# Earlier row copies, six products of zeros and an earlier request for small row transfers in a fused scan and two-layer network kernel

## The chip, the cores and the metric

The kernel runs on one core of a Trainium2 chip. The metric is device time in microseconds, from several executions, of which the median is given; the lower the better. A profiled execution records what each engine did and when: TensorE (PE, products, with its weight loads as PEld), VectorE (DVE), ScalarE (ACT), GpSimd (POOL) and SyncE (SP), which issues the DMA transfers.

## The reference

Three computations stand in a row: a gated linear recurrence over 768 tokens (4 batches, 8 heads, head dimension 32, state 16), a network with token mixing (1024 wide, squared ReLU, a sigmoid gate), and a second network (2048 wide, with h - tanh(h)).

```python
log_a = np.log(np.clip(a, 1e-06, 1.0))
cum = np.cumsum(la, axis=-1)                       # within a chunk
L = np.exp(cum[:, :, :, None] - cum[:, :, None, :]) * causal
M = np.einsum('bhin,bhjn->bhij', Cc, Bc) * L
y = M @ x + (C @ state) * exp(cum)                 # per chunk
state = decay_full * state + sum(B x decay_from_j)
...
xk = mu_k * x + (1.0 - mu_k) * x_prev;  xr = mu_r * x + (1.0 - mu_r) * x_prev
k = np.maximum(xk @ w_k, 0.0);  v = k * k @ w_v
r = 1.0 / (1.0 + np.exp(-(xr @ w_r)));  x = r * v
...
h = x @ w_in;  g = h - np.tanh(h);  out = g @ w_out
```

The third line and those with `y` and `state` are written short here.

## The kernel before

**Tiling.** The recurrence works in 12 groups of 256 tokens (4 chunks of 64 for all 8 heads). For a group k TensorE makes the exponents of the decays (`decays`, tile pd, line 442, for groups 0 and 1 line 438), ScalarE their exp (`decays_exp`, tile L), TensorE the score products (`scores`, pcb, L484), VectorE their product with the decays (`mask`, L544), TensorE the part that comes from the carried state (`inter`, L494), the state's additions (`terms`, L509) and the part within the chunk (`intra`, L516). VectorE carries the state on (`chain`, L558 and L561) and makes the scaled inputs bp (`weigh`, L457) and cp (`group_scale`, L428). ScalarE or VectorE copies the finished group from PSUM into xall (`group_out`). Both networks then work on 6 blocks of 512 tokens; each product is made as three products of high and low parts. The first network starts while the recurrence still runs.

**Weights.** The weights come as 64-bit numbers, 512 KB in one transfer (`fetch`, tile raw, L315), and are decoded into a high and a low part: one ScalarE square (keep, L322), four VectorE steps on raw and wd (L326, L329, L332, L335), a copy (wkh and the like, L364 or L366) and a subtraction (L341). There are two raw buffers; the first two fetches (W0 and W1 in the prediction, both from w_k) stand in the prologue.

**Decays of later groups.** The exponents of group k (from 2 on) are one product of `sr[:, k % 2]` with `rr[:, k % 2]`, 116 rows deep. Parts of both are fixed: sr is filled by GpSimd (`t_still`), and rows 0 to 111 of the two slots of rr by ScalarE (`causal`, then `spread`, one copy of 1024 columns each). The rest are rows of cumulated sums, which VectorE computes and SP writes out to `dcum`; `rows(k)` reads them back into sr and rr with two transfers (L399, L400). `prep_rows` reads such rows into kl (L404), from which TensorE (`scales_sum`, pc, L416) and an exp (er, L419) make the factors for cp and for the carried state (the carries).

**Order.** Each engine works its instructions off in the order in which they are written. The prologue's order is the list START, whose names stand for small functions: `W` is a weight fetch, `Db2` loads the third group's bct, `pr0` is `prep_rows` for the first batch's third group, `still` the fill of sr, `r0t` and `r0b` the copies into slot 0 of rr, `wa` 48 products of zeros on TensorE (`fill`, from the tile quiet), `d1` and `e1` the second group's decays and their exp, `sc1` its scores, `v0` the first group's visit (`inter`, `terms`, `intra`). All behind it is ordered by a greedy planner (`Plan.run`): each task has engines with modelled times, tasks that it follows, buffers (`Ring`) and a rank, and the planner always takes the task that can start first, among those ready the one of lowest rank. START_AT gives the time at which each engine is free in that model. The copies into slot 1 of rr are a planner task there, `filled` (2 ScalarE copies, rank of group 2), ahead of group 3's decays; `rows(2)` is one too. The first two blocks' decode is taken as ready from the model's start.

Of the kernel before, what the change touches and what calls it, by code (L numbers as in the profile page):

```python
# [16 lines left out]
P = 128  # L17
NB, NH, S, HD, NS = 4, 8, 768, 32, 16
NQ = NH // 2
L = 64  # L20
# [38 lines left out]

START = """  # L60
    qz tab Da Dla Dca Db0 Dx0 Db1 Dx1 Dnk Dnr seg mk wa c0t c1t c0b st mk2 tri
    cA lA cC lC sA ss h0s x0a cD lD x0b c1b ps pe d0 e0 dec dexp sD cum W Db2 W s0 x1a w0 x1b p0 m0 ob u0 h0 w1
    still heads r0t r0b spread sc1 d1 e1 v0 pr0 nu
""".split()

START_AT = dict(P=15.8, A=14.2, V=13.8, G=12.0, S=12.0, X=0.0, Y=0.0, Z=0.0)


def t_act(n, more=0.0):
    return 0.172 + n / 1200 + more
# [135 lines left out]
def chain_kernel(ctx, tc, xb, a, an, a0, bc, mu_k, mu_r, w_k, w_v, w_r, w_in, w_out, out):  # L208
# [14 lines left out]
    att = att_stack.enter_context(tc.tile_pool(name="att", bufs=1, side="right"))  # L223
    dram = ctx.enter_context(tc.tile_pool(name="dram", bufs=1, space=bass.MemoryType.DRAM))

    def fill(n):

        for _ in range(n):
            PE.matmul(acc[:, 0, 0:P], quiet, quiet, start=True, stop=True)  # L229

    def bank(name, shape=(2, BLK)):
        return pairs.tile([P, *shape], F32, tag="pair", name=name)
# [14 lines left out]
    dec = const.tile([P, NG, NQ, NC4], F32, name="dec")  # L247
    sums = const.tile([P, NU2 + 1], F32, name="sums")
    ones = const.tile([P, 1], F32, name="ones")
    quiet = const.tile([P, P], BF16, name="quiet")  # L250
    less = const.tile([P, NU2 + 1], F32, name="less")
    flag = const.tile([1, 1], I32, name="flag")

# [32 lines left out]
    for _ in range(NE):  # L286
# [2 lines left out]
    plan = Plan()  # L289
    add = plan.add  # L290
    R = dict(
        pair=Ring(3, ("pd", 1), ("pcb", 1), ("py", 0)), xb=Ring(3, 0, 1), bc=Ring(3, 0, 1, 2), rows=Ring(2, 0, 1), L=Ring(2, 0, 1), bp=Ring(2, 0, 1), cp=Ring(2, 0),
        er=Ring(2, 0), state=Ring(3, 0, 1), raw=Ring(2, *range(NW)), x=Ring(WORK["xh"]), l=Ring(WORK["l"], "p0"), h=Ring(WORK["h"], "p0", "p1"),
        s=Ring(WORK["s"], "p0"), acc=Ring(1), ob=Ring(3), raw2=Ring(2), f=Ring(WORK["f"], "p0", "p1"), wd=Ring(1), keep=Ring(2), wd2=Ring(1), keep2=Ring(2),
    )
# [102 lines left out]
    def rows(k):  # L398
        nc.sync.dma_start(out=f(sr[CUM:TOK, k % 2]), in_=dcum[k].rearrange("h x q c i -> (x q c) h i"))  # L399
        nc.sync.dma_start(out=f(rr[ROW:NR, k % 2]), in_=dcum[k].rearrange("h x q c i -> (h x) (q c) i"))  # L400

    def prep_rows(b, lo=0):
        d = dcum[NGB * b + lo // GT:NGB * (b + 1)].rearrange("k h x q c i -> (h x q) k (c i)")
        nc.sync.dma_start(out=f(kls[b % 2][TOK:ROW, lo:]), in_=d)  # L404
# [27 lines left out]
    def decays(k):  # L432
        pd = pds[k] = bank("pd")
        mt[k] = att.tile([P, 2, 2, NC4, L], F32, tag="L", bufs=2, name="L")
        if k < 2:
            for g in range(2):
                by = early["by", k][:, 2 * g:2 * g + 2].rearrange("p q c i -> p (q c i)")
                PE.matmul(pd[:, g], early["st"][:, k].rearrange("p h j -> p (h j)"), by, start=True, stop=True)
            return
        for g in range(2):  # L440
            by = rr[:, k % 2, 2 * g:2 * g + 2].rearrange("p q c i -> p (q c i)")
            PE.matmul(pd[:, g], sr[:, k % 2].rearrange("p h j -> p (h j)"), by, start=True, stop=True)
# [124 lines left out]
    def prologue(fetch1):  # L567
# [49 lines left out]
        def spread(out, lo, hi, cols, e):  # L617
            n = cols.stop - cols.start
            return lambda: copy(e, out[lo:hi], mk[lo:hi, cols].unsqueeze(2).to_broadcast([hi - lo, n, out.shape[-1]]))

        def causal(out, e):
            return lambda: copy(e, out[0:L], mk[0:L, 0:L].unsqueeze(1).to_broadcast([L, CQ, L]))

        def slot(k):
            return rr[:, k].rearrange("p q c i -> p (q c) i")
# [72 lines left out]
            V.memset(tbias, T2)  # L698
            G.memset(xall[:, :, 0:NB * (S + 1)].rearrange("p c (b s) -> p c b s", b=NB)[..., 0:1], 0.0)

        def rest():
            causal(slot(1), "A")()
            spread(slot(1), CUM, ROW, late, "A")()

        early["fill"] = rest
        fns = dict(
            qz=lambda: V.memset(quiet, 0.0), wa=warm(48), wc=warm(2), wd=warm(2), seg=t_seg,
            mk=t_mk, mk2=t_mk2, st=t_st, tri=t_tri, still=t_still, heads=t_heads, spread=t_spread,
# [1 line left out]
            c0t=causal(by[0], "V"), c1t=causal(by[1], "V"), c0b=spread(by[0], CUM, TOK, soon, "A"), c1b=spread(by[1], CUM, TOK, soon, "A"),  # L710
            h0s=spread(heads0.rearrange("p k (m n) -> p (k m) n", n=NS), CUM, TOK, pick, "A"),
            r0t=causal(slot(0), "A"), r0b=spread(slot(0), CUM, ROW, late, "A"),
            nu=t_nu,
            Da=load(ad, a0), Dla=load(la, a), Dca=load(ca, an), Dnk=load(mus["k"], mu_k), Dnr=load(mus["r"], mu_r), W=fetch1,
            Db0=lambda: bc_load(0), Db1=lambda: bc_load(1), Db2=lambda: bc_load(2), Dx0=lambda: xb_load(0), Dx1=lambda: xb_load(1),
# [3 lines left out]
            p0=lambda: scores(0), d0=lambda: decays(0), e0=lambda: decays_exp(0, True), d1=lambda: decays(1), e1=lambda: decays_exp(1, True),  # L719
            ps=scales0, pe=scales1, w0=lambda: weigh(0), w1=lambda: weigh(1), ob=lambda: out_bank(-1),  # L720
            u0=lambda: terms(0), m0=lambda: mask(0, True), h0=lambda: chain(0), s0=lambda: group_scale(0), sc1=lambda: scores(1), v0=lambda: visit(0),
            pr0=lambda: prep_rows(0, 2 * GT),
        )
        for o in START:
            fns[o]()
# [2 lines left out]
    def attention():  # L728

        D, E, MK, CH, GS, BPt, X, XL, BL, PSX, PS = ({} for _ in range(11))  # L730
        users = []

        def put(*args, **kw):
            t = add(*args, **kw)
            users.append(t)
            return t

        def at(k):
            return RANK_T * k

        def scales(b, lo, rank, after):
            take = [(R["pair"], ("pc", b))] + ([(R["er"], b)] if b else [])
            p = put(dict(P=0.62), lambda e: scales_sum(b, lo), after, rank, take, ins=4)
            PSX[b] = put(dict(A=t_act(S - lo)), lambda e: scales_exp(b, lo), [p], rank, uses=[take[0], (R["er"], b)], func="exp")
            return p

        PS[0] = scales(0, 2 * GT, at(2) - 2, [])
        E[1] = put(dict(Y=14.1), lambda e: None)
        filled = put(dict(A=2 * t_act(1024)), lambda e: early["fill"](), [], at(2))
        first_half, visited = None, put(dict(Z=14.8), lambda e: None)  # L750
        for k in range(1, NG + 1):
            if 2 <= k < NG:
                XL[k] = put(dict(S=0.47), lambda e, k=k: xb_load(k), [], at(k - 1.5), [(R["xb"], k)], dma=1.7)
                if k >= 3:
                    BL[k] = put(dict(S=0.47), lambda e, k=k: bc_load(k), [], at(k - 1.8), [(R["bc"], k)], dma=1.7)
                rw = put(dict(S=0.9), lambda e, k=k: rows(k), [], at(k - 1.2), [(R["rows"], k)], dma=0.2)
                D[k] = put(dict(P=0.7), lambda e, k=k: decays(k), [rw, filled if k == 3 else None], at(k) - 1.5, [(R["pair"], ("pd", k)), (R["L"], k)], [(R["rows"], k)], ins=4)
                E[k] = put(dict(A=t_act(1024)), lambda e, k=k: decays_exp(k), [D[k]], at(k) - 1.5, (), [(R["pair"], ("pd", k)), (R["L"], k)], func="exp")
                BPt[k] = put(dict(V=t_dve(GT)), lambda e, k=k: weigh(k), [XL[k]], at(k) - 1.5, [(R["bp"], k)], [(R["xb"], k)], port=True)
            b, g = divmod(k, NGB)  # L760
            if g == 0 and k < NG:
                pr = put(dict(S=0.45), lambda e, b=b: prep_rows(b), [PS.get(b - 2)], at(k - 1.2), (), dma=0.2)
                PS[b] = scales(b, 0, at(k) - 1.7, [pr])
            if k >= 2:
                j = k - 1
                take = ([(R["pair"], ("pcb", k))] if k < NG else []) + [(R["pair"], ("py", j))]
                use_a = [(R["cp"], j), (R["state"], j), (R["bc"], k)]
                use_b = [(R["pair"], ("py", j)), (R["L"], j), (R["xb"], j), (R["bp"], k), (R["xb"], k)]
                first_half = put(dict(P=(1.7 if j % NGB else 1.6) if k < NG else 0.65), lambda e, j=j: visit_a(j), [CH[j], GS[j], BL.get(k), D.get(k), PS.get(b) if k < NG else None, MK[j]], at(j), take, use_a, ins=192 if k < NG else 128)
                pause = put(dict(X=PAUSE), lambda e: None, [first_half])  # L770
                visited = put(dict(P=1.3 if k < NG else 0.8), lambda e, j=j: visit_b(j), [pause, XL.get(j), XL.get(k), BPt.get(k)], at(j), (), use_b, ins=192 if k < NG else 128)
            if k == NG:
                X[j] = put(dict(A=t_act(BLK), V=t_dve(BLK)), lambda e, j=j: group_out(j, e), [visited], at(j), (), [(R["pair"], ("py", j))])
                break
            MK[k] = put(dict(V=t_dve(1024)), lambda e, k=k: mask(k), [first_half, E.get(k)], at(k), (), [(R["pair"], ("pcb", k)), (R["L"], k)])
            CH[k] = put(
                dict(V=0.32 * moves(k)), lambda e, k=k: chain(k), [visited, PSX[b] if k > 1 else None], at(k) - 0.5,
                ([] if g else [(R["state"], k)]) + ([(R["state"], k + 1)] if g < NGB - 1 else []),
                [(R["pair"], ("py", k - 1)), (R["er"], b)] + ([(R["state"], k)] if g else []), port=True,
            )  # L780
            X[k - 1] = put(dict(A=t_act(BLK), V=t_dve(BLK)), lambda e, j=k - 1: group_out(j, e), [CH[k]], at(k - 1), (), [(R["pair"], ("py", k - 1))])
            GS[k] = put(dict(V=t_dve(BLK)), lambda e, k=k: group_scale(k), [BL.get(k), PSX[b] if k > 1 else None], at(k) - 0.5, [(R["cp"], k)], [(R["bc"], k), (R["er"], b)], port=True)
        return X, users
# [363 lines left out]
```

## Time and profile before

| | us |
|---|---|
| median of 3 runs | 493.2 (492.31 to 494.13) |
| profiled execution | 493.6 |
| span from its first to its last instruction | 491.4 |
| TensorE busy, share of the span | 474.5, 97% |
| VectorE busy | 399.6, 81% |
| ScalarE busy | 296.3, 60% |
| GpSimd busy | 8.5, 2% |

A busy TensorE is not a TensorE at its peak, since its products overlap and it counts as busy at either clock level; the granted clock is therefore read beside it. All of GpSimd's work lies in the first 11 us. In the rows below, an instruction's row gives its start and duration in us, the engine, the line of the kernel, the operation, output and inputs, their shapes, and the count where neighbours are merged; in square brackets stands the idle time of its engine ahead of it and what ended that. A row of busy times by stretch gives the stretch and its length, then busy time and instruction count of PE, PEld, DVE, ACT and POOL, then the granted clock of TensorE as a share of 2.4 GHz, the busy share of the 16 DMA engines and GB/s.

### The profile page before, as it was taken

How to read it: one execution, taken by the hardware profiler on the slowest of the kernel's cores; microseconds unless marked ns; L12 is line 12 of the kernel's file. 1: busy time of each engine (PE TensorE's matmuls, PEld its weight loads, DVE VectorE, ACT ScalarE, POOL GpSimd, SP SyncE). 2: the span in 40 equal slices, each digit the busy share in tenths (PEclk: the TensorE clock that was granted, in tenths of full speed). 3: DMA queues.
4: the chain of work that ended last, by engine and by line, in shares of the span. 5: the costliest groups of instructions: out<-in, count | busy, mean ns of one | idle time of the engine just before them, and what ended most of it. 6: DMA issues, size and time to landing. Idle time of an engine off the chain costs nothing.

```text
span 491.4 us, 9552 instructions
## 1 busy us (share of the span) xinstructions
PE 474.5 (97%) x4099; PEld 383.3 (78%) x4099; DVE 399.6 (81%) x504; ACT 296.3 (60%) x376; POOL 8.5 (2%) x27
## 2 busy tenths in 40 slices
PE   8789999999999999999999999999999999999993
PEld 6467778877878888877788788888878888887882
DVE  7799999999579999987877868767876966887582
ACT  7676978864657677747464554645465365455541
POOL 6000000000000000000000000000000000000000
PEclk9878999999999999999999999999999999999998
DMA  6773452221012322300000100100010010001001
GB/s 190 248 259 118 155 181 82 90 69 35 3 64 69 91 81 86 95 35 0 1 0 1 43 1 0 45 1 0 1 43 1 0 43 1 0 1 43 2 0 49
DMA packets 14120, 27.32 MB, mean 56 GB/s; under 512 B 2256, under 2 KB 3152, under 8 KB 14072
## 3 DMA queue, kind: packets, MB, share of 16 engines
q1 hardware_dynamic: 14072, 26.65, 17.0%
q8 instruction: 34, 0.56, 0.4%
q14 instruction: 14, 0.11, 0.1%
HBM read 23.30 MB, written 3.34 MB: 54 GB/s over the span
## 4 chain that ended last, share of the span: by engine, by line
PE 86%; DVE 8%; ACT 3%; DMA 1%; issue 1%; ACTq 0%; SPq 0%; DVEq 0%
PE acc L801 13%; PE acc L803 12%; PE acc L802 12%; PE ph L794 8%; PE ph L791 8%; PE ph L792 8%; PE pk L791 4%; PE pk L792 4%; PE pk L794 4%; PE pcb L484 2%; PE py L494 2%; PE py L516 1%; DMA raw<-in_w_k 1%; PE acc L229 1%; PE py L509 1%; PE pr L794 1%
## 5 line engine op out<-in xcount | busy, mean ns | idle before, releaser
L920 ACT ACTIVATE s<-ph 128x1024 f32<-128x1024 f32 (+1 forms) x49 | 49.5, 1009 | 66.8 <-PE ph L794 66.8
L925 DVE SCALAR_TENSOR_TENSOR f<-f,s 128x1024 f32<-128x1024 f32 (+1 forms) x49 | 58.8, 1200 | 30.1 <-ACT f L921 30.0
L364 ACT ACTIVATE h<-f 128x1024 fp32r<-128x1024 f32 (+1 forms) x44 | 45.8, 1041 | 51.4 <-DVE f L929 48.1
L791 PE MATMUL ph<-xh,winh 128*128 128x512 f32 x192 | 74.7, 389 | 0.0
L792 PE MATMUL ph<-xh,winl 128*128 128x512 f32 x192 | 74.7, 389 | 0.0
L938 DVE TENSOR_TENSOR l<-f,h 128x1024 fp32r<-128x1024 f32 (+1 forms) x49 | 58.9, 1202 | 18.6 <-ACT h L364 18.0
L801 PE MATMUL acc<-h,wouth 128*128 128x512 f32 x188 | 73.6, 392 | 0.3
L803 PE MATMUL acc<-l,wouth 128*128 128x512 f32 x188 | 73.4, 391 | 0.3 <-DVE l L938 0.2
L802 PE MATMUL acc<-h,woutl 128*128 128x512 f32 x188 | 73.2, 389 | 0.0
L929 DVE TENSOR_TENSOR f<-ph,f 128x1024 f32<-128x1024 f32 (+1 forms) x49 | 58.9, 1201 | 3.7 <-DVE f L925 0.5
L794 PE MATMUL ph<-xl,winh 128*128 128x512 f32 x192 | 59.2, 390 | 0.4 <-DVE xl L908 0.4
L921 ACT ACTIVATE f<-s,biases 128x1024 f32<-128x1024 f32 (+1 forms) x49 | 55.7, 1137 | 1.6
L794 PEld LDWEIGHTS ph<-xl,winh 128*128 128x128 f32 x192 | 36.0, 188 | 8.2 <-DVE xl L908 0.8
L801 PEld LDWEIGHTS acc<-h,wouth 128*128 128x128 f32 x188 | 35.3, 188 | 9.0 <-ACT f L921 1.5
L792 PEld LDWEIGHTS ph<-xh,winl 128*128 128x128 f32 x192 | 36.1, 188 | 7.5
L803 PEld LDWEIGHTS acc<-l,wouth 128*128 128x128 f32 x188 | 35.3, 188 | 8.5 <-DVE l L938 1.1
L791 PEld LDWEIGHTS ph<-xh,winh 128*128 128x128 f32 x192 | 36.0, 188 | 7.5
L802 PEld LDWEIGHTS acc<-h,woutl 128*128 128x128 f32 x188 | 35.3, 188 | 7.2
L791 PE MATMUL pk<-xh,wkh 128*128 128x512 f32 x96 | 39.0, 406 | 0.0
L801 PE MATMUL acc<-h,wvh 128*128 128x512 f32 x96 | 38.4, 400 | 0.0
L792 PE MATMUL pk<-xh,wkl 128*128 128x512 f32 x96 | 38.0, 396 | 0.0
L803 PE MATMUL acc<-l,wvh 128*128 128x512 f32 x96 | 37.6, 391 | 0.0
(135 smaller groups left out, 750.2 us busy)
## 6 DMA issues: line engine op xcount, KB each, us to landing
bct<-in_bc SPq DMA_DIRECT2D x12, 384.0 KB, 4.3
xbt<-in_xb SPq DMA_DIRECT2D x12, 384.0 KB, 4.6
raw<-in_w_in SPq DMA_DIRECT2D x8, 512.0 KB, 3.8
raw<-in_w_out SPq DMA_DIRECT2D x8, 512.0 KB, 3.5
out<-ob SPq DMA_DIRECT2D x11, 256.0 KB, 2.1
raw<-in_w_k SPq DMA_DIRECT2D x4, 512.0 KB, 4.6
raw<-in_w_v SPq DMA_DIRECT2D x4, 512.0 KB, 3.9
raw<-in_w_r SPq DMA_DIRECT2D x1, 512.0 KB
```

What stands on the lines that cost most here:

```text
L364: A.activation(out=out, in_=in_, func=AF.Copy)
L791: PE.matmul(o, wh[:, k, ms], hi[:, k], start=k == 0, stop=False)
L792: PE.matmul(o, wl[:, k, ms], hi[:, k], start=False, stop=False)
L794: PE.matmul(o, wh[:, k, ms], lo[:, k], start=False, stop=k == 1)
L801: PE.matmul(acc[:, c], wh[:, k, cs], h[:, e], start=first, stop=False, skip_group_check=True)
L802: PE.matmul(acc[:, c], wl[:, k, cs], h[:, e], start=False, stop=False, skip_group_check=True)
L803: PE.matmul(acc[:, c], wh[:, k, cs], l[:, e], start=False, stop=last, skip_group_check=True)
L920: A.activation(out=s, in_=phs[j, i][:, e], func=AF.Square, accum_out=sums[:, c:c + 1])
L921: A.activation(out=qs[j, i][:, e], in_=s, func=AF.Square, scale=PA, bias=pbias)
L925: V.scalar_tensor_tensor(out=q, in0=q, scalar=PG, in1=s, op0=ALU.add, op1=ALU.mult)
L929: V.tensor_tensor(out=q, in0=phs[j, i][:, e], in1=q, op=ALU.mult)
L938: V.tensor_tensor(out=l[:, e], in0=qs[j, i][:, e], in1=f(h[:, e]), op=ALU.subtract)
```

## The change

The copies into slot 1 of rr (`r1t`, `r1b`) move from the planner's task `filled` into START, behind `spread` and ahead of `sc1 d1 e1`; the task and the wait for it go. `pr0` and a new `rw2` (`rows(2)`) are issued on SP between the first weight fetch and Db2, with `still` emitted between them, so that Db2 and the second weight fetch stand behind them; the planner no longer issues `rows(2)`, and group 2's decays have no task to follow. After `v0` TensorE gets `wf`: six products of zeros with 384 columns into acc, for which quiet becomes three times as wide. In the planner's model SP is free from 13.6 instead of 12.0, and `rows` has three entries held.

```diff
@@ START
-    cA lA cC lC sA ss h0s x0a cD lD x0b c1b ps pe d0 e0 dec dexp sD cum W Db2 W s0 x1a w0 x1b p0 m0 ob u0 h0 w1
-    still heads r0t r0b spread sc1 d1 e1 v0 pr0 nu
+    cA lA cC lC sA ss h0s x0a cD lD x0b c1b ps pe d0 e0 dec dexp sD cum W pr0 still rw2 Db2 W s0 x1a w0 x1b p0 m0 ob u0 h0 w1
+    heads r0t r0b spread r1t r1b sc1 d1 e1 v0 wf nu
...
-START_AT = dict(P=15.8, A=14.2, V=13.8, G=12.0, S=12.0, X=0.0, Y=0.0, Z=0.0)
+START_AT = dict(P=15.8, A=14.2, V=13.8, G=12.0, S=13.6, X=0.0, Y=0.0, Z=0.0)
...
-    def fill(n):
+    def fill(n, w=P):
 
         for _ in range(n):
-            PE.matmul(acc[:, 0, 0:P], quiet, quiet, start=True, stop=True)
+            PE.matmul(acc[:, 0, 0:w], quiet[:, 0:P], quiet[:, 0:w], start=True, stop=True)
...
-    quiet = const.tile([P, P], BF16, name="quiet")
+    quiet = const.tile([P, 3 * P], BF16, name="quiet")
...
-        ... rows=Ring(2, 0, 1), ...
+        ... rows=Ring(2, 0, 1, 2), ...
...
-        def rest():
-            causal(slot(1), "A")()
-            spread(slot(1), CUM, ROW, late, "A")()
-
-        early["fill"] = rest
...
+            r1t=causal(slot(1), "A"), r1b=spread(slot(1), CUM, ROW, late, "A"), wf=lambda: fill(6, 3 * P),
...
-            pr0=lambda: prep_rows(0, 2 * GT),
+            pr0=lambda: prep_rows(0, 2 * GT), rw2=lambda: rows(2),
...
-        filled = put(dict(A=2 * t_act(1024)), lambda e: early["fill"](), [], at(2))
...
-                rw = put(dict(S=0.9), lambda e, k=k: rows(k), [], at(k - 1.2), [(R["rows"], k)], dma=0.2)
-                D[k] = put(dict(P=0.7), lambda e, k=k: decays(k), [rw, filled if k == 3 else None], at(k) - 1.5, ...)
+                rw = None if k == 2 else put(dict(S=0.9), lambda e, k=k: rows(k), [], at(k - 1.2), [(R["rows"], k)], dma=0.2)
+                D[k] = put(dict(P=0.7), lambda e, k=k: decays(k), [rw], at(k) - 1.5, ...)
```

## Rows read from the trace of the kernel before

**Rows 1.** Busy times of the engines in three stretches, with granted clock

```profile
17.77:21.45 3.68, 1.06 (x3) 0.48 (x3) 2.42 (x8) 3.31 (x5) 0.00 (x0) 0.86 0.56 171
20.70:30.70 10.00, 9.25 (x255) 7.16 (x256) 8.47 (x16) 6.27 (x11) 0.00 (x0) 0.50 0.71 200
48.80:482.00 433.20, 432.12 (x3196) 351.77 (x3197) 357.79 (x419) 261.93 (x325) 0.00 (x0) 1.00 0.12 39
```

**Rows 2.** Chain of waits up to 55 us: start, duration, what, count

```profile
0.94 0.11 DVE quiet L707
...
1.09 5.30 PE acc L229 x48
...
21.45 1.98 PE pcb L484 x32
...
28.44 5.40 DMA raw<-in_w_k
...
48.83 1.10 PE pcb L484 x32
...
51.15 0.23 PE pk L792
```

**Rows 3.** ScalarE in order of time, 15 to 22 us

```profile
15.54 1.09 ACT L453 ACTIVATE L<-pd 128x512 f32<-128x512 f32 x2 [2.16 <-PE pd L438]
...
18.10 0.66 ACT L322 ACTIVATE keep<-raw 128x512 f32<-128x512 f32 x1 [0.76 <-DMA raw<-in_w_k]
18.67 2.10 ACT L364 ACTIVATE rr<-s 64x1024 fp32r<-64x1024 f32 x2
20.80 0.60 ACT L364 ACTIVATE xall<-py 128x512 f32<-128x512 f32 x1
21.29 0.38 ACT L419 ACTIVATE er<-pc 128x256 f32<-128x256 f32 x1
```

**Rows 4.** TensorE in order of time, the products pc and pd of group 2

```profile
18.38 0.35 PE L416 MATMUL pc<-kl,heads 16*128 16x256 f32 x1 [0.63 <-DMA kl<-dcum]
19.48 0.70 PE L442 MATMUL pd<-rr,sr 116*128 116x512 f32 x2 [0.75 <-DVE wd L326]
```

**Rows 5.** VectorE in order of time, 19 to 36 us

```profile
19.28 0.42 DVE L457 TENSOR_TENSOR bp<-xbt,dec 128x256 f32<-128x256 f32 x1
19.61 0.68 DVE L329 SCALAR_TENSOR_TENSOR wd<-raw,wd 128x512 uint32<-128x512 uint32 x1
21.70 0.69 DVE L428 TENSOR_TENSOR cp<-bct,er 128x512 f32<-128x512 f32 x1 [1.41 <-ACT er L419]
...
26.36 0.69 DVE L428 TENSOR_TENSOR cp<-bct,er 128x512 f32<-128x512 f32 x1 [0.35 <-ACT er L419]
...
35.84 0.69 DVE L341 TENSOR_TENSOR wvl<-keep,wvh 128x512 fp32r<-128x512 f32 x1 [0.58 <-ACT wvh L364]
```

**Rows 6.** SP's issues of transfers in order of time, 9 to 13 us

```profile
9.49 0.50 SPq L315 DMA_DIRECT2D raw<-in_w_k  x1
10.05 0.45 SPq L393 DMA_DIRECT2D bct<-in_bc  x1
10.54 0.43 SPq L315 DMA_DIRECT2D raw<-in_w_k  x1
11.22 0.34 SPq L404 DMA_DIRECT2D kl<-dcum  x1
11.60 0.52 SPq L389 DMA_DIRECT2D xbt<-in_xb  x1
12.22 0.58 SPq L399 DMA_DIRECT2D sr<-dcum  x1
```

**Rows 7.** GpSimd in order of time, fills of sr

```profile
7.38 1.92 POOL L370 TENSOR_SCALAR_AFFINE_SELECT sr<-sr 64x256 fp32r<-64x256 f32 x3
```

**Rows 8.** DMA issues: count, KB each, us to landing; at 11.6 and 20.9 us

```profile
xbt<-in_xb SPq DMA_DIRECT2D x1, 384.0 KB, 7.5
...
kl<-dcum SPq DMA_DIRECT2D x1, 48.0 KB, 3.2
```

More of the change, by code (lines that the diff above doesn't have):

```diff
@@ L291, in chain_kernel @@
     R = dict(
-        pair=Ring(3, ("pd", 1), ("pcb", 1), ("py", 0)), xb=Ring(3, 0, 1), bc=Ring(3, 0, 1, 2), rows=Ring(2, 0, 1), L=Ring(2, 0, 1), bp=Ring(2, 0, 1), cp=Ring(2, 0),
+        pair=Ring(3, ("pd", 1), ("pcb", 1), ("py", 0)), xb=Ring(3, 0, 1), bc=Ring(3, 0, 1, 2), rows=Ring(2, 0, 1, 2), L=Ring(2, 0, 1), bp=Ring(2, 0, 1), cp=Ring(2, 0),
         er=Ring(2, 0), state=Ring(3, 0, 1), raw=Ring(2, *range(NW)), x=Ring(WORK["xh"]), l=Ring(WORK["l"], "p0"), h=Ring(WORK["h"], "p0", "p1"),
@@ L755, in attention @@
                     BL[k] = put(dict(S=0.47), lambda e, k=k: bc_load(k), [], at(k - 1.8), [(R["bc"], k)], dma=1.7)
-                rw = put(dict(S=0.9), lambda e, k=k: rows(k), [], at(k - 1.2), [(R["rows"], k)], dma=0.2)
-                D[k] = put(dict(P=0.7), lambda e, k=k: decays(k), [rw, filled if k == 3 else None], at(k) - 1.5, [(R["pair"], ("pd", k)), (R["L"], k)], [(R["rows"], k)], ins=4)
+                rw = None if k == 2 else put(dict(S=0.9), lambda e, k=k: rows(k), [], at(k - 1.2), [(R["rows"], k)], dma=0.2)
+                D[k] = put(dict(P=0.7), lambda e, k=k: decays(k), [rw], at(k) - 1.5, [(R["pair"], ("pd", k)), (R["L"], k)], [(R["rows"], k)], ins=4)
                 E[k] = put(dict(A=t_act(1024)), lambda e, k=k: decays_exp(k), [D[k]], at(k) - 1.5, (), [(R["pair"], ("pd", k)), (R["L"], k)], func="exp")
```

## The prediction

> **What bounds the kernel now.** I read the busy time by stretch first. From 48.8 us to 482 us TensorE is busy 432.1 of 433.2 us [rows 1]: behind the ramp nothing can be gained but by starting earlier. So the question is what the change does to the ramp, and whether that arrives at 48.8 us. In the ramp TensorE is not the bound: in 17.77 to 21.45 it is busy for 1.06 of 3.68 us, and in 20.7 to 30.7 the granted clock is 0.50, its lower level of 1.2 GHz, while VectorE works 8.47 of the 10 us [rows 1].
>
> Then the chain of waits. It runs through 48 products of zeros (5.30 us from 1.09, released by the memset of quiet), through group 2's score products at 21.45, through a weight transfer of 5.40 us issued at 28.44, and enters TensorE for good at 48.83 [rows 2]. Why do the score products start only at 21.45? ScalarE's rows answer: they wait for the copy xall (20.80, 0.60 us), which queues behind two row copies (18.67, 2.10 us), which queue behind the square keep (18.10), which had waited 0.76 us for the second weight block [rows 3]. Behind xall come the exp er (21.29) and with it VectorE's one large hole, 1.41 us ahead of cp at 21.70 [rows 3, 5]. The next holes are 0.35 us (26.36) and 0.58 us (35.84) [rows 5]. VectorE's work between them fills the ramp, so its line is the bound there, and a hole that closes is a gain.
>
> **The change, part by part.**
>
> **Row copies.** The pair of 2.10 us leaves 18.67 and follows spread on ScalarE. There the queue idles 2.16 us until 15.54, for pd's second products [rows 3]. It goes from 13.38 to 13.38 + 2.10 = 15.48, so it costs nothing, with 0.06 us to spare. Without this cover the exp at 15.54 would be late by up to 2.10 us, and the mask on VectorE behind it by as much.
>
> **Wider quiet.** The memset of 64 words takes 0.11 us [rows 2]; it is 192 words now. Three times the row is 0.33, and no growth is 0, so +0 to +0.22 us; I take +0.11, the middle. The zeros that start TensorE wait for it, and the chain goes through them, so all up to 17.77 moves by 0.11, to 17.88.
>
> **Order of transfers.** SP issues W0 at 9.49 (0.50 us), then kl. kl reads what the cumulated sums wrote, and went at 11.22 [rows 6]; it can go no earlier now, and SP stands from 9.99 to 11.22. Queued behind that wait are sr and rr (the third group's decay rows), bc2, W1 and all that the planner issues. With 0.34 us for kl, 0.58 for sr, 0.34 (kl's) for rr, 0.45 for bc2 and some 0.05 between two, W1 is issued at about 13.15 instead of 10.54, 2.6 late, and xb2, 0.43 and 0.05 behind it, at 13.65 instead of 11.60, 2.0 late [rows 6]. sr has to wait for POOL's fills of its tile too: the last ends at 9.30 [rows 7], before SP gets there. What the three small ones gain is early landing: between 3.2 us, the quieter row, and 7.5 us, the loaded one [rows 8], after 11.22 and 11.6; that is 14.4 to 19.1, before TensorE asks for them below. bc2, issued 2.6 late as well, is read by the score products only, at 20 or so. Who loses: W1 landed just before 18.10 [rows 3, 6] and xb2 at 11.60 + 7.5 = 19.10 [rows 6, 8]. Bound for both: not later at all, since the same bytes stand ahead of them and these 7.5 us are mostly queue; or later by the whole issue delay, W1 at 20.7 and xb2 at 21.1. I take +0.45 (18.5 and 19.55), nearer to the lower end: the quieter landing took 3.2 us [rows 8], so of 7.5 some 4.3 were backlog, which absorbs a later issue of 2.6 as long as the engines don't run dry.
>
> **Products of zeros.** Six with 384 columns after the first group's visit. One with 128 columns took 5.30/48 = 0.11 us, one of 512 columns takes 0.23 [rows 2]; between them by columns 0.19, so 1.1 us for six (0.66 if width cost nothing, 2.0 if three times the row). TensorE has them from 17.88 to 19.0. pc follows, 0.35, and pd, 0.70 [rows 4]: done at 20.05. In the trace these two ended at 18.73 and 20.18, so the zeros hide behind work that waited anyway.
>
> **ScalarE afterwards.** keep for the second block from 18.5 to 19.2, xall to 19.8 (its input, VectorE's state chain, is ready by then), er to 20.15 (durations of [rows 3]). The score products start at the later of 19.8 and 20.05, 1.4 us ahead of 21.45.
>
> **VectorE afterwards.** Its order up to the hole ends at 19.61 + 0.68 = 20.29 [rows 5]. The memset makes all of it 0.11 later; bp, which reads xb2, goes at 19.55 instead of 19.28 and makes it 0.27 later, the 0.11 included: 20.56. er is there at 20.15, so cp starts at 20.6, not 21.70: 1.1 us earlier, the hole of 1.41 less 0.27. What is late next is VectorE's own work; the holes of 0.35 and 0.58 stay.
>
> **Sum.** -1.41 (hole) + 0.11 (memset) + 0.16 (xb2 beyond that) + 0 (copies, zeros) = -1.1 us. It reaches 48.83 if VectorE stays the bound to there. The weight transfer at 28.44 is released by VectorE's reading of the block before, so it shifts along. Of the profiled execution 493.6 us (span 491.4) that makes 492.5; this execution stands 0.4 above the median of 493.2, so I predict a median of 492.1.
>
> **The rivals.**
>
> **The clock stays up.** In the trace the clock fell after TensorE had done 1.06 of 3.68 us [rows 1]. Now that stretch is filled: 1.1 us of zeros, 0.35, 0.70, then scores. If it stays at 2.4 GHz through 20.7 to 30.7, the score products take about half of their 1.98 us [rows 2], and the later exp and copies are no longer waited for: VectorE's holes of 0.35 and 0.58 go too. VectorE's work is a floor, so the gain ends at 1.1 + 0.93 = 2.0 us: 491.2. Against it: after scores TensorE waits for VectorE again, and can fall back a few us later. The Trainium skill, in "TensorE: Matmul & The Clock Gate", Part 1, holds that the half rate is the default and activity releases it, which would be this rival, in full for as long as the products keep coming. The drop to 0.50 right behind the thin stretch agrees [rows 1]; whether six products of zeros suffice no row shows.
>
> **The burst lands late.** The transfers are later by their whole issue delay: xb2 at 21.1, W1 at 20.7. Then keep runs to 21.4, xall to 22.0, er to 22.35, and cp goes at 22.35 instead of 21.70 (by way of bp, 0.42, and the decode step, 0.68, at 22.2): the new wait is longer than the old hole, by 0.65 us, and the ramp ends later: 493.2 + 0.65 = 493.9, slower than before. It decides from the point where W1 lands later than 20.05 or xb2 later than 20.6, 2.0 and 1.5 us behind their landing now. For it: SP stands still for 1.2 us with no transfer behind W0. Against: the backlog reckoned above.
>
> **The new plan costs a decode step.** The planner orders the rest greedily by the times in its model; SP starts at 13.6 in it instead of 12.0 and 2 us of ScalarE work are gone, so every later choice may come out otherwise. If one weight block's decode (four steps of 0.68 on VectorE at least, [rows 5]) comes ahead of the mixing that the first block's products need, TensorE's start at 48.83 is 2.7 us later: 492.1 + 2.7 = 494.8, and with another such swap 497.5. A swap the other way gives as much back. For it: little slack on VectorE; against: ranks are unchanged, and the shift of about 1 us is less than a group's step.
>
> **It does nothing.** Something else holds the score products at about 21.4, such as the buffer order in PSUM or the exp of the decays: 493.0 to 493.3.
>
> **How the numbers follow.** Forecast 0.42; clock 0.20; late burst 0.14; bad plan 0.15; nothing 0.09. Before 490.7 (faster by over 0.5%, about what a measurement of this kernel tells from no change) lie the clock's case with a little luck in the plan, 0.13, and the forecast's with a good plan, 0.06: 0.19. Above 495.7 lies what of the bad plan costs more than one step or meets the late burst: 0.13. Within: 0.68. Range 490.3 to 495.2: the lower end is the clock's 491.2 less a swap of one step of 0.7 and a little, the upper the bad plan's 494.8 with half of the late burst's term; some 0.1 lies beyond each.
>
> **What would show it.** Right: ScalarE's four row copies in one run up to about 15.5, xall at 19.5 to 20, the score products at about 20, no hole of over 0.5 us ahead of cp, and TensorE steady from about 47.7. Wrong: the exp after the copies later than 15.7 (no cover); keep for the second block or bp waiting for their transfers beyond 20.6 (late burst); a granted clock of 1.00 through 21 to 30 (clock rival); the same ramp, but TensorE's steady start at 49 or later (plan).

## The result and the profile after

The changed kernel takes 497.32 us (median of 5 executions, 496.04 to 499.16) against 493.01 us (median of 5, 492.31 to 494.13) for the kernel before. The ratio is 1.0097, with a 95% interval of 1.0077 to 1.0117: slower by about 1%, 4.3 us. The profiled execution of the changed kernel took 499.16 us, with a span of 497.0 us. It is the longest of its five, so the terms below, which come from it, are larger than the median's 4.3 us.

From the page of the changed kernel, the granted clock in 40 slices of 12.4 us, in tenths:

```profile
PEclk9969799999999999999999999999999999999998
```

TensorE has one 7 in its clock behind the ramp, in the fifth slice, 49.7 to 62.1 us. Before, everything from 48.8 us on ran at 1.00 [rows 1]. The windows of that stretch (length, busy time of TensorE, weight loads, VectorE, ScalarE and GpSimd with instruction counts, granted clock, DMA share, GB/s) show what happened:

```profile
50.00:52.00 2.00, 0.07 (x4) 0.00 (x0) 2.00 (x4) 2.00 (x4) 0.00 (x0) 1.00 0.93 261
52.00:53.00 1.00, 0.42 (x32) 0.42 (x33) 1.00 (x2) 0.52 (x1) 0.00 (x0) 0.54 0.70 261
53.00:54.00 1.00, 1.00 (x55) 0.83 (x37) 1.00 (x3) 0.00 (x0) 0.00 (x0) 0.50 0.27 99
54.00:58.00 4.00, 4.00 (x10) 3.13 (x10) 1.48 (x2) 1.35 (x2) 0.00 (x0) 0.50 0.00 0
58.00:60.00 2.00, 2.00 (x89) 1.31 (x90) 0.00 (x0) 2.00 (x4) 0.00 (x0) 0.77 0.00 0
60.00:482.00 422.00, 420.84 (x3001) 342.41 (x2984) 346.01 (x400) 251.46 (x309) 0.00 (x0) 1.00 0.12 37
```

TensorE stands still from 50 to 52.6 us. By the means of these windows the clock is at its lower level of 1.2 GHz from about 52.1 to 58.9 us, although the engine is busy from 52.6 us on. From 60 us on nothing is lost: 1.16 us idle in 422.

What TensorE waits for stands in its order of time around that hole. The chain of before had its steady start at 48.83 [rows 2], with the score products pcb of group 5, which group 4's visit writes ahead of group 4's own products py:

```profile
47.03 0.62 PE L442 MATMUL pd<-rr,sr 116*128 116x512 f32 x2
...
48.97 1.10 PE L484 MATMUL pcb<-bct 32*64 32x128 f32 x32
52.58 1.18 PE L494 MATMUL py<-cp,st 32*32 32x64 f32 x64 [2.51 <-ACT L L453]
```

The products py of group 4 do not read L. They write a pair of PSUM banks. There are three pairs, dealt out in turn: here to pd of group 5 (47.03), to pk (behind it), to pcb of group 5 (48.97), and the fourth, py, gets the pair of pd back. That pair is free once ScalarE's exp L has read pd. ScalarE's order of time in the changed kernel:

```profile
46.23 2.03 ACT L836 ACTIVATE f<-pk 128x1024 f32<-128x1024 f32 x2
48.16 1.99 ACT L843 ACTIVATE f<-f 128x1024 f32<-128x1024 f32 x2
50.05 0.62 ACT L364 ACTIVATE wrh<-keep 128x512 fp32r<-128x512 f32 x1
50.57 1.04 ACT L364 ACTIVATE h<-f 128x1024 fp32r<-128x1024 f32 x1
51.51 1.01 ACT L453 ACTIVATE L<-pd 128x1024 f32<-128x1024 f32 x1
```

And in the kernel before, the same exp and the products that need its bank:

```profile
47.76 1.02 ACT L841 ACTIVATE f<-pk 128x1024 f32<-128x1024 f32 x1
48.66 1.03 ACT L453 ACTIVATE L<-pd 128x1024 f32<-128x1024 f32 x1
...
49.86 0.85 PE L494 MATMUL py<-cp,st 32*32 32x64 f32 x64
```

Before, the exp ended at 49.69 and the products went at 49.86: 0.17 us to spare, less the 0.06 that a release takes (in the changed kernel 52.52 to 52.58). After, the exp has two ReLUs, two squares and two copies ahead of it and ends at 52.52. The order of TensorE's instructions is the same in both kernels, but for the products of zeros that were added; ScalarE's differs in its first 64 instructions only, and this exp is one of the last to stand elsewhere. VectorE's differs in its first 100, and one copy of xall has gone from ScalarE to it.

The profiled executions differ by 5.6 us of span. Group 5's score products start 0.14 us later (48.97 for 48.83), the wait is 2.51 us, and the clock costs about 3.1 us: by the windows above 0.46 + 0.50 + 4 x 0.50 + 2 x 0.23 = 3.4 us of full clock are missing in 52 to 60, less 0.3 for the 0.58 us in which TensorE still waited. The sum is 5.7 us.

The clock's part isn't the same in every execution. Experiment e2 (below) has the same wait of 2.51 us, and its profiled execution (497.22 us) lies beside its median. The same window in the changed kernel, then in e2:

```profile
52.00:60.00 8.00, 7.42 (x162) 5.70 (x164) 3.48 (x5) 3.88 (x6) 0.00 (x0) 0.57 0.12 45
```

```profile
52.00:60.00 8.00, 7.21 (x168) 5.71 (x169) 4.33 (x8) 4.05 (x6) 0.00 (x0) 0.79 0.15 48
```

At 0.79 the eight microseconds lack 1.7 us of full clock, at 0.57 they lack 3.4. With 1.7 for the clock, 0.14 and 2.51 make about 4.3 us, as much as the medians differ by. What the parts are worth by themselves, the experiments tell.

In the ramp the hole that was to close, 1.41 us ahead of cp [rows 5], is still there. ScalarE and VectorE of the changed kernel:

```profile
12.83 2.12 ACT L364 ACTIVATE rr<-s 64x1024 fp32r<-64x1024 f32 x2
14.98 1.08 ACT L453 ACTIVATE L<-pd 128x512 f32<-128x512 f32 x2
...
19.18 0.66 ACT L322 ACTIVATE keep<-raw 128x512 f32<-128x512 f32 x1 [2.39 <-DMA raw<-in_w_k]
19.75 0.37 ACT L419 ACTIVATE er<-pc 128x256 f32<-128x256 f32 x1
20.01 0.59 ACT L364 ACTIVATE xall<-py 128x512 f32<-128x512 f32 x1
```

```profile
20.15 0.69 DVE L428 TENSOR_TENSOR cp<-bct,er 128x512 f32<-128x512 f32 x1 [1.35 <-ACT er L419]
```

The two row copies run early and in nobody's way. But keep now waits 2.39 us for the second weight block, where it waited 0.76 [rows 3], and holds er and cp behind it. SP's issues from 11.5 us on, against [rows 6]:

```profile
11.55 1.42 SPq L399 DMA_DIRECT2D sr<-dcum  x1
13.02 0.32 SPq L400 DMA_DIRECT2D rr<-dcum  x1
13.39 0.36 SPq L393 DMA_DIRECT2D bct<-in_bc  x1
13.80 0.43 SPq L315 DMA_DIRECT2D raw<-in_w_k  x1
14.27 0.47 SPq L389 DMA_DIRECT2D xbt<-in_xb  x1
```

### The profile page after: what moved, and what is told of

The parts are those of the page before. It is cut to its first block, busy times and chain, and to the rows that moved or that the text cites. A ratio compares the mean times of both kernels' runs of the same rounds, so it can differ in the third digit from the quotient of the medians.

```text
span 497.0 us, 9565 instructions
## 1 busy us (share of the span) xinstructions
PE 476.4 (96%) x4105; PEld 383.6 (77%) x4105; DVE 400.6 (81%) x505; ACT 296.0 (60%) x375; POOL 8.4 (2%) x27
## 3 DMA queue, kind: packets, MB, share of 16 engines
q1 hardware_dynamic: 14072, 26.65, 16.8%
## 4 chain that ended last, share of the span: by engine, by line
PE 75%; DVE 13%; ACT 4%; DMA 3%; issue 2%; POOL 1%; SPq 1%; ACTq 0%; POOLq 0%; DVEq 0%
PE acc L796 12%; PE acc L798 11%; PE acc L797 11%; PE ph L789 8%; PE ph L786 8%; PE ph L787 8%; PE pk L786 3%; PE pk L789 3%; PE pk L787 3%; DVE wd L332 2%; DVE wd L329 1%; PE py L494 1%; PE pcb L484 1%; DVE l L819 1%; PE py L516 1%
## 5 line engine op out<-in xcount | busy, mean ns | idle before, releaser
L364 ACT ACTIVATE h<-f 128x1024 fp32r<-128x1024 f32 (+1 forms) x43 | 44.7, 1039 | 50.4 <-DVE f L924 47.8
L933 DVE TENSOR_TENSOR l<-f,h 128x1024 fp32r<-128x1024 f32 (+1 forms) x49 | 58.9, 1201 | 18.6 <-ACT h L364 18.0
L924 DVE TENSOR_TENSOR f<-ph,f 128x1024 f32<-128x1024 f32 (+1 forms) x49 | 58.9, 1201 | 3.3
L797 PE MATMUL acc<-h,wvl 128*128 128x512 f32 x96 | 38.0, 396 | 0.0
```

The lines of the kernel that those rows point to most:

```text
L364: A.activation(out=out, in_=in_, func=AF.Copy)
L797: PE.matmul(acc[:, c], wl[:, k, cs], h[:, e], start=False, stop=False, skip_group_check=True)
L924: V.tensor_tensor(out=q, in0=phs[j, i][:, e], in1=q, op=ALU.mult)
L933: V.tensor_tensor(out=l[:, e], in0=qs[j, i][:, e], in1=f(h[:, e]), op=ALU.subtract)
```

## The experiments

Three theories stood. **Start**: the later transfers, copies or zeros of the prologue themselves cost the time. **Order**: the planner, whose model was changed along with the prologue, writes another order for what follows, and that costs it. **Exp**: of this order it is the one late exp.

Medians are in us. The ratio is to the kernel before on the same chip (493.05 to 493.3 us there). The last two columns come from one profiled execution each: the start of cp, and that of group 5's score products, both less the end of the first group's products. That end itself moves by 1 us between executions (last section), so I subtract it.

| run | median (lowest to highest, executions) | ratio, 95% | to cp | to group 5's scores |
|---|---|---|---|---|
| before | 493.01 (492.31–494.13, 5) | 1 | 3.94 | 31.07 |
| after | 497.32 (496.04–499.16, 5) | 1.0097 [1.0077, 1.0117] | 3.33 | 32.15 |
| e1_new_start_old_order | 493.81 (492.37–495.44, 12) | 1.0012 [0.9996, 1.0027] | 5.32 | 31.58 |
| e2_old_start_new_order | 497.19 (497.11–497.22, 4) | 1.0087 [1.0059, 1.0115] | 3.87 | 32.26 |
| e3_one_exp_earlier | 493.86 (492.17–495.83, 12) | 1.0019 [1.0001, 1.0037] | 2.79 | 31.79 |
| e4_no_zeros | 496.75 (495.03–498.60, 6) | 1.0082 [1.0055, 1.0109] | 2.84 | 31.86 |
| e5_copies_alone | 492.25 (490.45–494.23, 12) | 0.9977 [0.9958, 0.9995] | 2.82 | 30.16 |
| e6_transfers_alone | 493.78 (492.83–496.39, 12) | 1.0018 [0.9997, 1.0039] | 5.39 | 32.24 |
| e7_copies_new_order_exp_moved | 492.70 (491.88–493.64, 12) | 0.9988 [0.9971, 1.0005] | 1.89 | 30.57 |
| e8_copies_rows_behind_block | 491.98 (491.03–493.73, 12) | 0.9980 [0.9964, 0.9996] | 2.83 | 29.44 |
| e9_old_start_exp_moved | 494.19 (493.10–495.58, 10) | 1.0020 [1.0004, 1.0036] | 3.87 | 33.06 |
| e10_zeros_in_the_wait | 495.67 (494.94–497.18, 9) | 1.0057 [1.0040, 1.0074] | 3.15 | 31.88 |
| e12_model_sp_12 | 496.68 (495.15–497.65, 6) | 1.0065 [1.0043, 1.0087] | 3.61 | 31.00 |

### The prologue with the old order, and the old prologue with the new one

The first kernel is the changed one with the planner's model of before: two of its tasks come back empty, so that the order behind the prologue is that of before.

```diff
-START_AT = dict(P=15.8, A=14.2, V=13.8, G=12.0, S=13.6, ...)
+START_AT = dict(P=15.8, A=14.2, V=13.8, G=12.0, S=12.0, ...)
-rows=Ring(2, 0, 1, 2)
+rows=Ring(2, 0, 1)
+filled = put(dict(A=2 * t_act(1024)), lambda e: None, [], at(2))
-rw = None if k == 2 else put(dict(S=0.9), lambda e, k=k: rows(k), ...)
+rw = put(dict(S=0.9), lambda e, k=k: rows(k) if k > 2 else None, ...)
-D[k] = put(dict(P=0.7), lambda e, k=k: decays(k), [rw], ...)
+D[k] = put(dict(P=0.7), lambda e, k=k: decays(k), [rw, filled if k == 3 else None], ...)
```

> The prologue of the changed kernel with the planner's model and tasks of the kernel before (a task without work stands for the row copies and for the third group's rows), so that behind the prologue every engine has the order of before. Theory A (the loss is the planner's new order on ScalarE and VectorE, the prologue's edits themselves gain): 493.0 - 1.1 = about 491.9, score products at about 20.2, no stretch at half clock behind 50 us. Rival B (the late second weight block and what waits for it costs, whatever the order): 496 to 498.

The second is the kernel before with the planner's model of the changed one; the two copies are emitted from the first square of the decoding and group 2's rows from its xb load, beside which they stood before.

```diff
-START_AT = dict(P=15.8, A=14.2, V=13.8, G=12.0, S=12.0, ...)
+START_AT = dict(P=15.8, A=14.2, V=13.8, G=12.0, S=13.6, ...)
-rows=Ring(2, 0, 1)
+rows=Ring(2, 0, 1, 2)
+            if n == 1:
+                early["fill"]()
+        if k == 2:
+            rows(2)
-        filled = put(dict(A=2 * t_act(1024)), lambda e: early["fill"](), [], at(2))
-                rw = put(dict(S=0.9), ...)
+                rw = None if k == 2 else put(dict(S=0.9), ...)
-                D[k] = put(..., [rw, filled if k == 3 else None], ...)
+                D[k] = put(..., [rw], ...)
```

> The reverse: transfers, row copies and TensorE's work of the prologue as before (no products of zeros, the row copies behind the second square, the third group's rows behind its xb), but the planner's order of the changed kernel on every engine. Theory A: as slow as the change or slower, 497 to 499, with TensorE waiting some 2.5 us for an exp of the decays at about 52 to 54. Rival B: 493 as before.

Measured: 493.81 and 497.19 us. The changed prologue without the new order costs 0.6 us by the ratio, and its interval takes in no cost (1.0012 [0.9996, 1.0027]). It doesn't gain the 1.1 us that were expected either. The new order without the changed prologue costs the whole loss. Its TensorE has the same wait, with the same length:

```profile
52.79 1.00 PE L498 MATMUL py<-cp,st 32*32 32x64 f32 x64 [2.51 <-ACT L L457]
```

Start falls as the cause of the loss, order stands.

### One exp put back

The changed kernel with a single instruction moved: group 5's exp is emitted behind its products and falls between the two ReLUs, instead of behind the copy h.

```diff
-D[k] = put(dict(P=0.7), lambda e, k=k: decays(k), ...)
+D[k] = put(dict(P=0.7), lambda e, k=k: (decays(k), decays_exp(k) if k == 5 else None), ...)
-E[k] = put(dict(A=t_act(1024)), lambda e, k=k: decays_exp(k), ...)
+E[k] = put(dict(A=t_act(1024)), lambda e, k=k: decays_exp(k) if k != 5 else None, ...)
```

> The changed kernel with one ScalarE instruction moved: the exp of group 5's decays goes right behind its products, between the two ReLUs ahead of it, instead of behind two ReLUs, two squares and two copies; all else keeps its order. Theory A1 (this one late exp is the loss: 2.5 us of wait ahead of 52.6 and some 3 us of half clock behind it): 497.3 - 5 = about 492, granted clock 1.00 from 50 us on. Rival A2 (the loss is spread over the many swaps of the new order): 495 or more, though that wait is gone.

Measured: 493.86 us, 3.5 us less than the changed kernel; about 5 were expected, from the terms of its longest execution. ScalarE and TensorE of this run:

```profile
45.89 1.02 ACT L836 ACTIVATE f<-pk 128x1024 f32<-128x1024 f32 x1
47.39 1.03 ACT L453 ACTIVATE L<-pd 128x1024 f32<-128x1024 f32 x1 [0.47 <-PE pd L442]
48.32 1.02 ACT L836 ACTIVATE f<-pk 128x1024 f32<-128x1024 f32 x1
```

```profile
48.68 1.10 PE L484 MATMUL pcb<-bct 32*64 32x128 f32 x32
49.71 0.85 PE L494 MATMUL py<-cp,st 32*32 32x64 f32 x64
```

The products follow the score products without a wait, and the granted clock is 1.00 in every window from 50 us on. The time equals that of the changed prologue with the old order, 493.81: on this prologue the other differences of order cost nothing that shows.

e9 is e2 with this same edit:

```diff
-D[k] = put(..., lambda e, k=k: decays(k), [rw], ...)
+D[k] = put(..., lambda e, k=k: (decays(k), decays_exp(k) if k == 5 else None), [rw], ...)
```

> e2_old_start_new_order (prologue's work of before, planner's order of the change; 497.2) with the one exp of group 5's decays moved up as in e3_one_exp_earlier. Theory A1 (that one place is the whole loss of the new order, whatever the prologue does): 493.0 to 494.0, no wait of the py products for it near 52 us. Rival A2 (the other swaps of the new order cost something of their own, which the prologue of the change hid): 495 or more.

Measured: 494.19 us, 3.0 less than e2's 497.19. So the one exp carries most of the loss on either prologue. On the old one 1.1 us of it stays (1.0020 [1.0004, 1.0036]), and its group 5's score products come latest of all, 33.06 us behind the first group's products. What of that order costs it, VectorE's part of it or another, was not tried.

### The wait and the clock taken apart

The changed kernel with 12 products of zeros, 384 columns wide, behind the call of group 5's score products, where TensorE stands still. The wait stays; only the engine is kept at work in it.

```diff
 ...
+    if k == 4:
+        fill(12, 3 * P)
```

> The changed kernel with twelve more products of zeros (384 columns, some 2.3 us), put where TensorE waits for the late exp, ahead of its py products at 52.6 us; the exp stays late. What the loss is made of: if the wait of 2.5 us is all, 497 to 498; if half of it is the stretch at half clock behind the wait (53 to 59 us, 6 us at half clock, some 3 us of work), the stretch goes, the granted clock stays 1.00 and 494 to 495.

Measured: 495.67 us, between the two forecasts. TensorE, and two windows:

```profile
50.02 2.12 PE L229 MATMUL acc<-quiet 128*128 128x384 bf16 x12
52.59 0.85 PE L494 MATMUL py<-cp,st 32*32 32x64 f32 x64 [0.44 <-ACT L L453]
```

```profile
52.00:56.00 4.00, 3.56 (x77) 2.87 (x76) 3.48 (x5) 1.47 (x3) 0.00 (x0) 1.00 0.21 73
56.00:60.00 4.00, 4.00 (x101) 3.18 (x100) 1.64 (x5) 4.00 (x7) 0.00 (x0) 1.00 0.33 97
```

The products come at 52.59 as before the edit (52.58), but the clock stays at 2.4 GHz. So the lower clock is worth 1.65 us by the medians (497.32 - 495.67), 2.0 by the ratios (1.0097 - 1.0057, of 493), and 3.1 between the two profiled executions (499.16 and 496.05), of which the first is the long one. The wait itself is the rest to e3: 1.8 us (495.67 - 493.86), less than the 2.51 of its row. Of the 3.5 us that e3 gets back about half is the clock, which falls behind an idle stretch and stays down while TensorE is at work again. The Trainium skill, in "TensorE: Matmul & The Clock Gate", Part 1, holds that the half rate is the default and work releases it. The pair agrees: 0.50 with 2.51 us of wait, 1.00 with the same wait filled.

### One number of the planner

The new order comes from three edits of the model together: SP's start, the missing task of 2 us on ScalarE and the missing task of group 2's rows. With any one of them set back, the order that the planner writes has the exp between the second ReLU and the square again, as before. Only one of the three was run, SP's start:

```diff
-START_AT = dict(P=15.8, A=14.2, V=13.8, G=12.0, S=13.6, ...)
+START_AT = dict(P=15.8, A=14.2, V=13.8, G=12.0, S=12.0, ...)
```

> The changed kernel with SP free from 12.0 in the planner's model, as before, instead of 13.6; everything else of the change is in it. In this order the exp of group 5's decays stands ahead of the second square again. Theory A1: 493.0 to 494.2, the whole loss turns on that one number. Rival A2: 495 to 497.

Measured: 496.68 us. The exp runs at 47.73, the wait of 2.51 us is gone, group 5's score products come 1.1 us earlier than in the changed kernel, and the time is nearly the same. Here TensorE's order is another one too: products of acc and pk change places. Its windows:

```profile
60.00:70.00 10.00, 9.15 (x190) 6.90 (x171) 9.76 (x19) 6.78 (x9) 0.00 (x0) 1.00 0.40 136
70.00:80.00 10.00, 9.05 (x198) 7.01 (x191) 9.53 (x17) 6.67 (x9) 0.00 (x0) 1.00 0.60 182
80.00:100.00 20.00, 18.66 (x168) 14.51 (x167) 18.69 (x28) 15.77 (x18) 0.00 (x0) 1.00 0.22 61
```

TensorE idles 0.85 + 0.95 + 1.34 = 3.1 us in 60 to 100, all at full clock, where the kernel before idled at most 1.08 us from 48.8 to 482 [rows 1]. The idle time consists of many short waits, such as this:

```profile
71.88 0.47 PE L786 MATMUL pk<-xh,wkh 128*128 128x512 f32 x1 [0.47 <-DVE xh L366]
```

I had taken this for a repair, and it is another order with another loss. The exp theory says what the changed kernel lost, not that the next plan loses nothing.

### The parts of the prologue alone

e5 is the kernel before with the copies moved and nothing else, the transfers as they were:

```diff
-    still heads r0t r0b spread sc1 d1 e1 v0 pr0 nu
+    still heads r0t r0b spread r1t r1b sc1 d1 e1 v0 pr0 nu
```

> The kernel before with one part of the change: the two row copies in the prologue, behind spread. Transfers, their order, and the order behind the prologue on every engine are those of before; no products of zeros. Theory C (the copies' gain is real, and the late second weight block gave it back): the block lands at 18.1 as before, xall at 19.1 to 19.7, cp at 20.3 to 20.7 instead of 21.7, 491.7 to 492.1. Rival D (the hole ahead of cp closes, but the ramp ends no earlier, since something further on is late anyway): 492.8 to 493.3 with cp at 20.3 to 20.7.

Measured: 492.25 us, 0.9977 [0.9958, 0.9995]: faster by 1.05 us by the medians. ScalarE and VectorE:

```profile
13.38 2.12 ACT L364 ACTIVATE rr<-s 64x1024 fp32r<-64x1024 f32 x2
15.53 1.09 ACT L453 ACTIVATE L<-pd 128x512 f32<-128x512 f32 x2
...
18.10 0.66 ACT L322 ACTIVATE keep<-raw 128x512 f32<-128x512 f32 x1 [0.76 <-DMA raw<-in_w_k]
19.12 0.60 ACT L364 ACTIVATE xall<-py 128x512 f32<-128x512 f32 x1 [0.36 <-DVE st L561]
```

```profile
20.20 0.68 DVE L428 TENSOR_TENSOR cp<-bct,er 128x512 f32<-128x512 f32 x1
```

e6 has the new order of the transfers, and the copies where they were:

```diff
-    sD cum W Db2 W s0 ...
+    sD cum W pr0 still rw2 Db2 W s0 ...
-    still heads r0t r0b spread sc1 d1 e1 v0 pr0 nu
+    heads r0t r0b spread sc1 d1 e1 v0 nu
```

> The kernel before with the other part: kl and the third group's rows asked for ahead of its bct and the second weight block; the row copies stay behind the second square, no products of zeros, order of before. Theory C: the second block lands at some 20.4, the copies run 21.1 to 23.2, xall to 23.8, cp at some 24.2 instead of 21.7, and 495.0 to 495.6. Rival D: the ramp takes it up, 493.0 to 494.0, though cp is at 24.

Measured: 493.78 us, 0.5 us slower than before, with an interval from 0.15 faster to 1.9 slower; 495.0 or more were expected. VectorE:

```profile
22.34 0.69 DVE L428 TENSOR_TENSOR cp<-bct,er 128x512 f32<-128x512 f32 x1 [1.61 <-ACT er L419]
```

cp comes 5.39 us behind the first group's products, where it came 3.94 behind them before. e6 alone can't be told from no cost. The pair of e1 and e5 can: with both parts, in e1, the time is 493.81 against 492.25 with the copies alone, and the intervals don't meet. So the copies are worth about a microsecond, and asking for the rows ahead of the weight block takes it back. (e1 has the products of zeros as well, which cost nothing that shows in e4.)

e8 puts the rows behind the second weight block and ahead of xb2, with the copies moved:

```diff
-    sD cum W Db2 W s0 ...
+    sD cum W Db2 W pr0 still rw2 s0 ...
-    still heads r0t r0b spread r1t r1b sc1 d1 e1 v0 pr0 nu
+    heads r0t r0b spread r1t r1b sc1 d1 e1 v0 nu
```

> As e5_copies_alone, but kl and the third group's rows stand right behind the second weight block, ahead of the third group's xb (which is issued some 1 us later). Theory C: 491.7 to 492.1, if xb still lands by 19.5; if it lands at 20 or later, bp waits for it on VectorE and half of the gain goes. Rival D: 492.8 to 493.3.

Measured: 491.98 us, 0.9980 [0.9964, 0.9996]. With e5 it is one of the two that beat both kernels; the two cannot be told apart. The block is not late (keep starts at 17.60), and group 5's score products come earliest of all, 29.44 us behind the first group's products. That is 0.7 us ahead of e5; by the medians it is 0.3, which they cannot tell from nothing.

e7 is e3 without the transfers' order and the zeros of the change:

```diff
-    sD cum W pr0 still rw2 Db2 W s0 ...
-    heads r0t r0b spread r1t r1b sc1 d1 e1 v0 wf nu
+    sD cum W Db2 W s0 ...
+    still heads r0t r0b spread r1t r1b sc1 d1 e1 v0 pr0 nu
+        if k == 2:
+            rows(2)
```

> The changed kernel with its late exp moved as in e3_one_exp_earlier, the transfers of the prologue in the order of before, and no products of zeros: row copies in the prologue and the planner's new order. Theory C: 493.9 less what the late block cost, 491.5 to 492.5. Rival D: 493.5 to 494.

Measured: 492.70 us, 0.9988 [0.9971, 1.0005]. It lies between e5 and the kernel before and is told from neither. The new order with its exp put back has nothing to offer over the old one.

### No zeros

```diff
-    heads r0t r0b spread r1t r1b sc1 d1 e1 v0 wf nu
+    heads r0t r0b spread r1t r1b sc1 d1 e1 v0 nu
```

> The changed kernel without the six products of zeros (the wider memset stays). If they hide and change no clock: 497.3 within 0.5, the wait at 52 us unchanged. If they hold the clock up behind the first visit: a granted clock of 0.50 from some 20 us on, as in the kernel before, and 0.5 to 1.5 us longer. If they delay what follows: up to 1.1 us shorter.

Measured: 496.75 us against 497.32, intervals overlapping by most of their length. The zeros neither cost nor bring what can be told. Nor do the traces show that they hold the clock up longer: in 22 to 24 us the mean grant was 1.00 with them in the changed kernel and 0.66 without them in e4, but 0.65 with them in e3 and 1.00 without them in e8.

## Why the prediction was wrong, by its steps

**What failed: the reach to 48.83.** The sum ended with the sentence that the ramp's gain reaches TensorE's steady start if VectorE stays the bound to there. It did not: behind the steady start TensorE waited 2.51 us for ScalarE, and then ran at the lower clock. The forecast of 492.1 rested on an order of work that the change had altered: e2, with the new order and nothing else, takes 497.19 us. The sum had no term for that order; the runs put it at 3.5 us (e3): 1.8 of wait and 1.65 of clock.

Without the new order the forecast would have missed too, by less: e1 took 493.81 us and not 492.1, because the term for the transfers was too small (below).

**The rival that came true: the new plan.** It was given 0.15, and 494.8 us, 497.5 with a second swap. The kind of cause is right. Its place and price are not: I put the swap on VectorE, a weight block's decode ahead of a mixing step, because VectorE's line bounded the ramp. It was an exp on ScalarE, an engine with 60% of busy time, and it counted because of what it held: one of three pairs of PSUM banks, 0.17 us before TensorE needed it. The price left out the clock, about half of the 3.5 us by e10. That the second figure, 497.5, lies so near to the measured 497.32 is chance: no decode step on VectorE made it. The argument against it, that ranks are unchanged and the shift is small, was wrong: with the same ranks the exp went from ahead of the second square to behind both squares and two copies, and ended 2.8 us later.

**Row copies.** Right. Forecast: run from 13.38, the exp behind them at 15.54 not delayed, cp 1.1 us earlier. In e5: 13.38, 15.53, and cp 2.82 us behind the first group's products instead of 3.94, 1.1 earlier (in the executions' own times 20.20 for 21.70, 1.5 earlier). The median gained 1.05 us.

**Order of transfers.** The mechanism was right and the size was off. The second block was forecast to be issued at 13.15 and to land at 18.5, with bounds of 18.1 and 20.7. It was issued at 13.80, because sr's issue took 1.42 us and not 0.58, and landed at 19.18. In e1 it landed at 20.45 and in e6 at 18.74, all inside the bounds and above the value taken. The term of +0.16 for the later transfers, all of it for xb2, is the one that was mis-sized. In e6 they made cp 1.5 us later (5.39 for 3.94; 0.6 in the executions' own times, 22.34 for 21.70), by way of the block, keep, the copies and er, and e1's median is 1.6 us above e5's. That is more than the copies bring. I had reckoned that a backlog of 4.3 us absorbs the delay; issued 2.2 to 3.3 us later, the block landed 0.5 to 2.4 us later.

**The late burst** as a rival was reckoned at 493.9 us, with cp behind bp at 22.35 once the block lands at 20.7. e1's profiled execution, the longest of its twelve, is that case: the block at 20.45, and

```profile
21.54 0.42 DVE L457 TENSOR_TENSOR bp<-xbt,dec 128x256 f32<-128x256 f32 x1 [2.41 <-DMA xbt<-in_xb]
...
22.49 0.68 DVE L428 TENSOR_TENSOR cp<-bct,er 128x512 f32<-128x512 f32 x1
```

cp at 22.49, and a median of 493.81 us. As an account of the ramp it deserved more than 0.14.

**Wider quiet.** The memset took 0.22 us, +0.11 as forecast. Its effect cannot be seen: the 48 products behind it vary by ten times that (last section).

**Zeros.** Right: six took 1.15 us (forecast 1.1) and hid ahead of pc; e4 shows no cost. The size had some luck. The 0.11 us for 128 columns was read at the lower clock and the 0.23 for 512 at the higher one; in the changed kernel the 48 products go 0.056 us apart once the clock is up (last section).

**The clock stays up.** It did not happen: in 20.7 to 30.7 the mean grant was 0.70 instead of 0.50 [rows 1], since the fall came within 24 to 26 us (0.69 there). No gain came with it; group 5's score products came 32.15 us behind the first group's products, not earlier than before.

**It does nothing.** Out, by e5 and by e2.

**What would show it.** Of the signs named, the copies in one run were seen, xall and the score products at about 20 were seen (20.01, 20.17), and the hole ahead of cp (1.35) spoke against the forecast. The late burst's own sign, a wait beyond 20.6, was not seen in the changed kernel (keep at 19.18). The sign for the plan was a steady start at 49 or later; it came at 52.58.

What could have been read beforehand: the exp's end at 49.69 and the products at 49.86 stood in the trace of before. I looked for VectorE's holes only, where something already waits, and not for the thin places, where a buffer is released just in time. The new order itself could have been read too, since the planner that writes it is part of the kernel.

## To carry to other kernels

Where a planner writes the order, an edit of its model is a change to the whole kernel: lay the instruction order of each engine beside the old one before any sum, and price each place that moved by the buffer it holds. Look in the trace for releases that come just before their buffer is used, on engines with time to spare too, and add to a new wait of TensorE the stretch at the lower clock that may follow it: it followed 2.51 us of wait here, and not the 0.44 us that were left in e10. The small transfers put ahead of a large one that is already waited for cost more here than the copies saved (e1 against e5); behind it (e8) they cost nothing that shows.

## What the runs showed of the hardware that was not expected

**Products of zeros at different speeds.** The 48 products at the start took 4.23 to 5.30 us in 13 profiled executions, and 4.30 in the changed kernel:

```profile
1.22 4.30 PE L229 MATMUL acc<-quiet 128*128 128x128 bf16 x48 [1.22 <-DVE quiet L702]
```

It was 5.30 before [rows 2]. With the two longest, 5.30 each, the first group's products end latest (17.38 in e5, 17.76 before, 16.8 to 17.2 in the others). The starts of the 48 show where the difference comes from: in the changed kernel the first 30 go about 0.107 us apart and the rest, from 4.3 us on, 0.056, about the ratio of the two clock levels; before, all 48 go about 0.107 apart. So it is the moment at which the clock rises that differs. What sets that moment is open.

**One slow issue on SP.** Most issues take 0.3 to 0.6 us, but between 9 and 32 us one or more took 1.0 to 1.9 in 11 of the 13 executions: sr 1.42 in the changed kernel, the second block itself in e1:

```profile
12.75 1.60 SPq L315 DMA_DIRECT2D raw<-in_w_k  x1
```

Where the slow one was the block's, the block landed latest (20.45 in e1, 19.30 in e10, with an issue of 1.59 there). Ahead of 15 us such an issue stands in all eight executions that issue sr and rr right behind kl, and in none of the five with xb2 between them. Why is open.

**Stops of TensorE that nothing releases.** In a run of equal products TensorE stops for 1.2 to 2.1 us in 6 of the 13 executions, put down to issue: 1.22 ahead of the products at 22.71 in the changed kernel, 1.41 at 22.52 in e4, 2.07 at 25.33 in e8. The kernel before has none of over 0.2 us. They go by the place in TensorE's stream and not by the product: in five executions 346 products are ahead of the stop, in e4 without the six zeros as well, and in e8 473, 127 more. What causes them was not tried.
